# One block with attention and a gated MLP on one Trainium2 core: LayerNorm 1's modulation on transposed x, half of V's lane-matched copies on engines, and a new written order

## The chip, the cores and the metric

The kernel runs on one core of one Trainium2 chip. The metric is device microseconds per execution. Before the change three executions took 297.26, 295.96 and 296.14 us; the median is 296.14 us. A separate, profiled execution took 296.91 us.

## The reference

Everything is bfloat16; x is 2048 tokens by 448 features. A small vector c gives six modulation rows of 448 (shift, scale and gate for each of two halves). The first half is causal attention in a window of 256 tokens with 16 heads of 28 features, the second a gated MLP in which one 2048 by 2048 matrix mixes the tokens.

```python
mod = silu(c) @ w_mod                  # 448 -> 6 rows: sa, ca, ga, sb, cb, gb
h = layernorm(x) * (1 + ca) + sa       # LayerNorm 1 and its modulation
q, k, v = split(h @ wqkv)              # 16 heads of 28
p = softmax(where(0 <= i - j < 256, q @ k.T * 28 ** -0.5, -1e9))
x = x + ga * ((p @ v) @ wo)
h = layernorm(x) * (1 + cb) + sb       # LayerNorm 2 and its modulation
z = gelu_tanh(h @ w_in)                # 1792 columns
z1, z2 = z[:, :896], layernorm(z[:, 896:])
out = x + gb * ((z1 * (w_sp @ z2 + b_sp[:, None])) @ w_out)
```

## The kernel before

The 2048 tokens are 16 tiles of 128 (t for keys and values, j for queries), and four tiles make a block (tb 0 to 3). All matmuls want their contracted dimension on the partitions, so normalised x is transposed into hT (four chunks of features by 2048 tokens).

**The order.** The function first lists every operation with the engines that may do it, its dependencies and a planner's cost. It does not search: a long string, ORDER, names each operation by its number of creation, its engine and its buffer slot, in order. Each engine runs its operations in exactly this order, so an operation that waits holds up all that stand behind it on that engine. SP (SyncE) issues nearly all transfers, in order as well. Planner costs only order the waits; nothing is timed by them on the chip.

**Front (up to about 20 us).** Matmuls with c (L557, L562) give the modulation columns. LayerNorm 1's modulation goes into the weights: `pad` multiplies the q and k weights by 1 + ca while it spreads heads to 32 columns (WQK, L609 and L610), wv is multiplied likewise (L636, L637), and the shift becomes a bias row: `bias` (L619) multiplies sa by the weights, and the result is put into the row of WQK and wv that meets a column of ones in xn. x is normalised to xn (L668, L670, L673) and transposed, for tb 0 and 1 by the TensorE (L718) and a copy to hT (L731, L732), for tb 2 and 3 by transposing transfers from xn to hT (L476). For tb 0 the four q groups are computed chunk by chunk (L746), then the k groups (L758). V comes from L806 into Vaug (copies L810, L811). For tb 3 K comes tile by tile (L793).

**Attention (to about 131 us).** For each query tile j and each half of the heads: scores on the TensorE (L901 for j 0 and 1; from j 2 on L931, L945 and, through QBD, L959), the exponential on ScalarE (L887, 128x2048 and 128x512), a mask product on VectorE (L964), and P times V (L985, called PV below). For j of 2 and more PV reads V from Vaug and also from VX, in which the 64-row halves of V's tiles are put together in four ways (VX index 0 to 3) so that a window's pieces of 64 keys meet. VX of block tb is used first by the PV of j = 4 tb (j = 2 for tb 0). Of its six pieces of 64 partitions, four stay on their partitions (index 0 and 2 on the lower half, 1 and 3 on the upper: lane-matched) and two cross over. All six are written by four transfers for each block (L826 to L829), two of which write two pieces each:

```python
(lambda e, ...: e.dma_start(both(vx(0, 0), 8 * row, n), both(vo(0, a, b), 0, n)), 0),      # L826: index 0 and 2
(lambda e, ...: e.dma_start(vx(0, 64), vo(0, a - 2, b - 2)), 2),                           # L827
(lambda e, ...: e.dma_start(vx(3, 0), vo(64, a, b)), 0),                                   # L828
(lambda e, ...: e.dma_start(both(vx(1, 64), 8 * row, n), both(vo(64, a - 2, b - 2), 0, n)), 2)  # L829: 1 and 3
```

After PV: a transpose (L1000), 1 / sum (L1002), the product (L1003), a transpose into hT (L1006), the output projection (L1010), x1 (L1015), LayerNorm 2, a transposing transfer (L476), modulation (L1035, L1037).

**Rest (131 to 295 us).** z2 (L1100) and z1 (L1146), the token mixing with w_sp, which is transposed by 32 transfers (L476, wspA and wspB; L1169), the bias and the product with z1 (L1173, L1176), the last projection (L1186), the residual (L1196) and one store for each tile (L1201).

Of the kernel before, what the change touches and what calls it, by code (L numbers as in the profile page):

```python
# [5 lines left out]
BF16 = mybir.dt.bfloat16  # L6
# [13 lines left out]
1.a 26.v 35.g 0.s 27.v 28.v 29.v 38.g 39.g 2.a 4.s 36.g 3.a 33.g 30.v 5.s 37.g 57.a 31.v 34.g 32.v 40.g 6.s 7.s 8.s 9.s 10.s 11.s 12.s 152.v 154.v  # L20
41.g 67.p.1 68.p.2 69.p.3 58.p.0 59.a 60.a 53.a 70.p.4 71.p.5 72.p.6 73.p.7 81.p.2 82.p.3 83.p.4 84.p.5 66.p.1 43.g 42.g 163.v 153.v 155.v 156.g 157.g
13.s 161.v 164.v 162.v 165.v 14.s 166.g 158.v 159.v.0 160.a.1 167.v 169.v.2 170.p.2 168.a.3 171.p 172.a 173.a 174.p.3 175.p 122.v 121.v 135.v 142.p.4
134.g 138.a 140.v 137.v 141.v 136.v 143.v 176.a 177.v 139.a 178.p.5.6.7.0 179.p 144.p.1 180.p 182.p 145.a 146.p.1 199.p.2 181.p 186.v 149.a 147.a
200.a 217.v 213.v 215.v 219.v 48.v 216.v 218.v 214.v 220.v 185.a 62.g 61.g 150.g 151.a 148.g 193.p.4 194.a 195.p.3 196.a 183.p 201.p.6 15.s 16.s 187.a
367.p.0 184.p 197.p.1 63.v 221.v 188.v 198.v 55.g 222.g 223.v 51.v 224.g.0 226.g.1 205.p.7 203.p.0 54.g 368.a 371.p.0 206.a 372.a 204.a 123.p.1 65.v
227.v.2 49.v 225.v.3 369.v 125.v 124.v 64.v 389.p.0 228.p.0 128.p.1 229.v 207.p.7 230.p.0 390.a 391.a 394.p.0 202.a 208.a 395.a 396.a 192.s 189.s
190.s 191.s 17.s 18.s 21.s 22.s 209.s 19.s 211.s 210.s 20.s 212.s 129.v 126.p.1 231.v 127.v 373.v 264.v 268.v 46.v 415.p.0 232.p.0 238.p.1 413.p.0
233.a 239.a 234.p.0 236.p.1 414.a.0 237.a 416.a 370.p.0 374.p 419.p.0 265.v 270.v 266.v 45.v 47.v 269.v 271.v 44.v 267.v 235.v 375.v.0 392.v 50.v
254.p.0 246.p.1 421.p.0 393.p.0 272.g 273.g 274.v 276.g.0 420.a.1 397.v 255.v 319.v 439.p.0 398.p 247.a 422.a 440.a.2 244.p.0 441.p.0 248.p.1 445.p.0
245.a 442.a 423.v 417.v 399.v.1 317.v 418.p.0 424.p 250.p.0 447.p.0 318.v 315.v 425.v.2 443.v 320.v 316.v 446.a.3 251.a 448.a 376.v 241.s 242.s 243.s  # L30
240.s 465.p.0 444.p.0 258.p.0 467.p.0 466.a.4 259.a 468.a 278.g.1 277.g.2 132.g 56.g 130.g 275.g.3 249.v 252.p.1 321.v 449.v 322.v 323.v 400.v 253.v
52.v 426.v 280.s 281.s 282.s 279.s 471.p.0 450.p 256.p.0 473.p.0 472.a.0 299.p.1 257.a 474.a 300.a 491.p.0 283.p.0 295.p.1 493.p.0 324.g 401.g.0
451.v.3 325.v 133.g 131.g 377.v.1 402.v 378.v 469.v 284.v 492.a.1 296.a 494.a 403.p.0 404.v 427.v.2 261.s 260.s 24.s 262.s 263.s 497.p.0 285.p.1
499.p.0 379.p.0 498.a.2 286.a 500.a 470.p.0 517.p.0 327.g.0 328.v.1 428.v 329.v.2 380.v 452.v 475.v 289.p.1 287.p.0 519.p.0 476.p 518.a.3 495.v 501.v
405.v 288.v 477.v.1 290.a 520.a 523.p.0 429.p.1 297.p.0 525.p.0 524.a.4 298.a 526.a 406.v 478.v 521.v 527.v 430.v 381.v 496.p.0 543.p.0 502.p 305.p.0
545.p.0 301.p.1 544.a.0 306.a 546.a 549.p.0 479.g.0 453.g.1 326.g.3 454.v 503.v.0 302.v 382.v 307.p.0 303.p.1 551.p.0 550.a.1 431.v 504.v 505.g.2
383.g 407.g 480.v 304.v 432.v 553.v 433.v 506.v 408.g 409.g 410.g.0 434.g 23.s 332.s 292.s 291.s 294.s 25.s 293.s 330.s 331.s 312.s 333.s 522.p.0
308.a 552.a 569.p.0 455.p.1 309.p.0 571.p.0 528.p 570.a.2 310.a 572.a 575.p.0 456.v 481.p.1 577.p.0 507.p.0 576.a.3 578.a 547.v 529.v.2 457.v 530.v
548.p.0 458.v 482.v 508.v 435.v 384.g 531.g.1 459.g 532.v 595.p.0 554.p 338.p.1 597.p.0 533.p.0 460.g 436.g.1 437.g 573.v 411.v 483.v 555.v.1 579.v
484.v 534.v 535.v 536.v 485.v 596.a.4 339.a 598.a 601.p.0 336.p.1 603.p.0 340.p.0 602.a.0 604.a 621.p.0 314.s 313.s 311.s 438.s 337.v 556.v 341.v  # L40
623.p.0 334.p.1 574.p.0 580.p 537.v 599.v 385.g 557.g.0 581.v.3 622.a.1 335.a 624.a 627.p.0 352.p.0 582.v 509.v 605.v 353.v 348.p.1 629.p.0 349.v
386.g.2 486.g 344.s 412.s 345.s 343.s 342.s 461.g 583.g.2 584.v 462.v.1 463.g 510.v 511.g 538.g 600.p.0 628.a.2 630.a 363.s 464.s 647.p.0 346.p.0
585.p.1 649.p.0 558.v 387.v 625.v 388.s 487.v 631.v 648.a.3 347.a 650.a 653.p.0 606.p 655.p.0 559.p.0 654.a.4 656.a 607.v.0 586.v 560.v 539.v 561.v
626.p.0 673.p.0 632.p 633.v.2 562.v 634.v 608.v 350.p.1 675.p.0 351.v 356.p.0 674.a.0 676.a 679.p.0 540.v.0 357.v 635.g.1 563.g 564.g 360.p.1 354.p.0
681.p.0 541.v 488.g.1 609.g.2 680.a.1 636.v 657.v 651.v 361.v 610.v 683.v 355.a 682.a 699.p.0 637.p.0 652.p.0 658.p 701.p.0 700.a.2 702.a 705.p.0
489.g 565.g 784.g 566.g.2 512.g 567.g 365.s 362.s 364.s 542.s 638.v 611.p.1 358.p.0 568.s 587.v 639.v 659.v.1 640.v 641.v 612.v 707.p.0 706.a.3 359.a
708.a 725.p.0 727.p.0 726.a.4 728.a 677.v 642.g 643.v 660.v 588.v 613.v 703.v 678.p.0 684.p 731.p.0 787.g 661.g.0 513.g 614.v 662.v 514.v.0 685.v.3
709.v 686.v 729.v 687.g.1 663.p.1 704.p.0 710.p 733.p.0 732.a.0 734.a 751.p.0 711.v.2 730.p.0 753.p.0 752.a.1 754.a 688.v 712.v 515.v 589.g 735.v
689.p.0 736.p 366.s 490.s 801.s 802.s 516.s 785.g 713.g.2 664.v 615.v 714.v 644.g.2 755.v 757.p.0 759.p.0 715.p.1 758.a.2 790.a 760.a 737.v.0 645.v
756.p.0 786.g 590.g 616.g 690.v 665.v 738.v 739.g.0 761.v 833.p.0 834.p.1 835.p 762.p 791.a 788.a 789.a 666.v 716.v 740.v 717.v 741.p.0 763.v.1 742.v  # L50
764.v 667.g 591.g 592.g.1 593.g 668.g 669.v 617.v 837.a 836.p 691.v 692.v 718.v 618.v.0 646.s 670.v.2 839.v 838.v 619.g 845.a 868.p.2 869.p.3 870.p
871.p 851.p.0 872.a 852.p.1 853.p 854.p 880.a 981.p.2 846.v 671.v 743.v 744.v 745.v 777.g 693.g 694.g 746.g 747.g 594.s 620.s 672.s 719.v 765.v.1
766.v 767.p.0 862.a 840.v 720.g 748.v.1 749.g 863.g 695.v 881.v 750.s 780.g 721.g 696.g.0 792.g 722.g.2 841.v 768.v 874.v 769.v 697.v 770.v 771.g
873.v 793.v 795.v 794.v 882.a.0 855.a 982.p.1 983.p 886.p.3 887.p.0 888.p 889.p 984.p 986.a 985.a 847.a.1 698.s 857.v 883.v 772.g 773.v 723.v 724.s
774.g.1 856.v 775.v 776.s 858.v 799.v 806.s 814.s 813.s 807.s 798.v 875.v 890.a 897.a 987.a 988.a 898.g 842.g 843.g 816.s 804.s 811.s 810.s 805.s
809.s 812.s 815.s 808.s 803.s 899.a.0 779.g 844.g 884.g 783.g 921.p.2 922.p.3 923.p 924.p 864.a.1 797.v 796.v 932.a 903.p.0 904.p.1 865.v 892.v 866.g
# [1212 lines left out]
```

## Time and profile before

| what | value |
|---|---|
| median of three executions | 296.14 us |
| the profiled execution: its time, and the span of its trace | 296.91 us, 295.0 us |
| busy: TensorE, VectorE, ScalarE, GpSimd | 271.4, 158.6, 139.2, 131.1 us |
| mean granted TensorE clock | 0.977 |
| front; attention; z1 and z2; token mixing and output | 0 to 20; 20 to 131.4; 131.4 to 173.5; 173.5 to 295.0 us |

PE is the TensorE, PEld its loading of weights, DVE VectorE, ACT ScalarE, POOL GpSimd, SPq the queue of SyncE. In the chain and in the timeline a line has a start, a duration (both in us), an engine or "issue" (time in which an engine waited for nothing that the profile shows), and the line of the program. An x4 behind it counts instructions. "[3.78 <-DMA VX<-Vaug]" is idle time ahead of an instruction and what ended it.

### The profile page before, as it was taken

How to read it: one execution, taken by the hardware profiler on the slowest of the kernel's cores; microseconds unless marked ns; L12 is line 12 of the kernel's file. 1: busy time of each engine (PE TensorE's matmuls, PEld its weight loads, DVE VectorE, ACT ScalarE, POOL GpSimd, SP SyncE). 2: the span in 40 equal slices, each digit the busy share in tenths (PEclk: the TensorE clock that was granted, in tenths of full speed). 3: DMA queues.
4: the chain of work that ended last, by engine and by line, in shares of the span. 5: the costliest groups of instructions: out<-in, count | busy, mean ns of one | idle time of the engine just before them, and what ended most of it. 6: DMA issues, size and time to landing. Idle time of an engine off the chain costs nothing.

```text
span 295.0 us, 8590 instructions
## 1 busy us (share of the span) xinstructions
PE 271.4 (92%) x3795; PEld 135.4 (46%) x3795; DVE 158.6 (54%) x360; ACT 139.2 (47%) x182; POOL 131.1 (44%) x179
## 2 busy tenths in 40 slices
PE   6999979599999785699999999999999999999995
PEld 2445444245555553344444444444444444444452
DVE  7688996828989697488785600013011024051534
ACT  3688989659999695488999950000000000000000
POOL 6563386006942385376884861006313064252310
PEclk9999999979999998599999999999999999999999
DMA  7927643964774959612399999940000000000123
GB/s 220 297 100 197 140 81 78 213 189 102 152 106 95 108 102 172 94 22 56 66 150 180 168 219 170 195 69 2 0 0 0 2 0 0 0 18 0 62 64 109
DMA packets 58959, 29.50 MB, mean 100 GB/s; under 512 B 48041, under 2 KB 56298, under 8 KB 58922
## 3 DMA queue, kind: packets, MB, share of 16 engines
q1 hardware_dynamic: 58376, 28.26, 48.3%
q10 hardware_dynamic: 546, 0.69, 0.8%
q8 instruction: 30, 0.49, 0.7%
q14 instruction: 7, 0.06, 0.1%
HBM read 9.01 MB, written 1.84 MB: 37 GB/s over the span
## 4 chain that ended last, share of the span: by engine, by line
PE 80%; DMA 6%; DVE 4%; issue 3%; ACT 3%; SPq 1%; POOL 1%; ACTq 0%
PE ps L1169 33%; PE ps L1100 7%; PE ps L1146 7%; PE ps L1186 7%; PE ps L758 5%; PE ps L985 5%; DMA VX<-Vaug 5%; PE ps L1010 4%; PE ps L806 3%; PE ps L931 2%; DMA wmod<-in_w_mod_dram 2%; ACT PW L887 2%; PE ps L959 2%; PE ps L945 1%; PE ps L746 1%
## 5 line engine op out<-in xcount | busy, mean ns | idle before, releaser
L887 ACT ACTIVATE PW<-ps 128x2048 bf16<-128x2048 f32 (+1 forms) x56 | 68.7, 1241 | 21.0 <-PE ps L945 14.1
L1176 POOL TENSOR_TENSOR z1T<-tmpg,z1T 128x512 bf16<-128x512 bf16 x28 | 31.8, 1152 | 77.0 <-DVE tmpg L1173 77.0
L1173 DVE TENSOR_TENSOR tmpg<-ps,bsp_bc 128x512 bf16<-128x512 f32 x28 | 19.0, 689 | 75.5 <-PE ps L1169 65.0
L1169 PE MATMUL ps<-wspB,z 128*128 128x512 bf16 x224 | 50.0, 379 | 0.0
L1169 PE MATMUL ps<-wspA,z 128*128 128x512 bf16 x224 | 49.5, 379 | 0.0
L1169 PEld LDWEIGHTS ps<-wspA,z 128*128 128x128 bf16 x224 | 21.9, 98 | 26.6 <-POOL z L1115 0.4
L1169 PEld LDWEIGHTS ps<-wspB,z 128*128 128x128 bf16 x224 | 21.9, 98 | 26.3
L1003 POOL TENSOR_TENSOR o_sb<-ou,rec_all 128x512 bf16<-128x512 f32 x13 | 15.5, 1198 | 38.3 <-DVE rec_all L1002 33.6
L758 PE MATMUL ps<-hT,WQK 128*128 128x512 bf16 x96 | 25.5, 400 | 0.0
L964 DVE TENSOR_TENSOR PW<-PW,mask 128x1024 bf16<-128x1024 bf16 x28 | 22.3, 808 | 1.2 <-ACT PW L887 1.2
L1100 PE MATMUL ps<-w_in,hT 64*128 64x448 bf16 x224 | 22.0, 349 | 0.4 <-ACT PW L887 0.4
L1146 PE MATMUL ps<-hT,w_in 64*128 64x512 bf16 x196 | 22.0, 376 | 0.0
L1186 PE MATMUL ps<-w_out_g,z1T 128*128 128x448 bf16 x112 | 21.8, 352 | 0.0
L656 POOL TENSOR_TENSOR rs_all<-ve_all,neghalf 128x1 f32<-128x1 f32 (+2 forms) x29 | 18.6, 646 | 3.9 <-DVE ve_all L653 3.2
L1196 DVE TENSOR_TENSOR fin<-ps,x_sb 128x448 bf16<-128x448 f32 x16 | 9.4, 620 | 18.5 <-PE ps L1186 16.8
L648 DVE BATCH_NORM_STATS2 st_all<-x_sb 128x6 f32<-128x448 bf16 x32 | 18.7, 605 | 0.0
L673 POOL TENSOR_SCALAR xn<-x_sb,rs_all,ve_all 128x448 bf16<-128x448 bf16 x18 | 17.3, 961 | 3.0 <-DVE ve_all L660 2.4
L985 PE MATMUL ps<-PW,VX 128*32 128x64 bf16 x896 | 14.3, 199 | 4.6 <-issue 4.5
L985 PE MATMUL ps<-PW,Vaug 128*32 128x128 bf16 x224 | 12.0, 231 | 6.0 <-DMA VX<-Vaug 6.0
L1000 DVE STREAM_TRANSPOSE ou<-ps 128x512 f32<-128x512 f32 x16 | 11.3, 708 | 10.9 <-PE ps L985 10.9
L1154 ACT ACTIVATE z1T<-ps 128x512 bf16<-128x512 f32 x28 | 14.8, 603 | 3.9 <-PE ps L1146 3.7
L1010 PE MATMUL ps<-wo_g,hT 128*128 128x448 bf16 x64 | 16.1, 374 | 0.2 <-issue 0.2
(130 smaller groups left out, 382.0 us busy)
## 6 DMA issues: line engine op xcount, KB each, us to landing
VX<-Vaug SPq DMA_DIRECT2D x6, 512.0 KB, 5.3
VX<-Vaug SPq DMA_DIRECT2D x8, 256.0 KB, 4.1
out_dram<-fin SPq DMA_DIRECT2D x16, 112.0 KB, 1.8
x_sb<-in_A_x_dram SPq DMA_DIRECT2D x3, 448.0 KB, 4.8
wmod<-in_w_mod_dram SPq DMA_DIRECT2D x1, 1344.0 KB, 8.7
w_in<-in_B_w_in_dram SPq DMA_DIRECT2D x1, 1344.0 KB, 10.3
QBD<-qT SPq DMA_DIRECT2D x16, 64.0 KB, 2.5
w_out_g<-in_B_w_out_dram SPq DMA_DIRECT2D x1, 784.0 KB, 5.7
```

The source lines that it names most:

```text
L648: st = [dve(0.62 if True else 0, lambda e, t=t, ci=ci, s=s: e.bn_stats(st_all[:, slot, t, ci, :], s()), deps(t), prio) for ci, s in enumer ...
L758: m = pe(4 * MMS, [lambda e, h=h, g=g, kc=kc, tb=tb: e.matmul(ps[:, h.slot[0], :], lhsT=WQK[:, kc, 4 * g:4 * g + 4, :].rearrange("p a b -> ...
L887: ex = act(xdur, lambda e, out_ap=out_ap, in_ap=in_ap: e.activation(out_ap(), in_ap(), ACT.Exp, scale=SCALE), [s], v - 8.0 + u, takes, tab ...
L964: fk = lambda e, at_w=at_w, cols=cols: e.tensor_tensor(cols(at_w(), [[512, 4], [128, 4], [1, 64]], PW), cols(at_w(), [[512, 4], [128, 4], ...
L985: fns.append(lambda e, hO=hO, hi=hi, qi=qi, V=V, of=of, q0=q0, w=w, first=bi == 0, last=bi == len(pieces) - 1: e.matmul(ps[32 * hi:32 * hi ...
L1010: mo = pe(4 * MMD, [lambda e, h=h, j=j, ch=ch: e.matmul(ps[:, h.slot[0], 0:D], lhsT=hT[:, ch, j * 128:(j + 1) * 128], rhs=wo_g[:, ch, :], ...
L1100: return lambda e, kc, p0, start, stop: e.matmul(ps[:, hs[t % 2].slot[hf], 0:D], lhsT=hT[p0:p0 + 64, kc, t * 128:(t + 1) * 128], rhs=w_in[ ...
L1146: return lambda e, kc, p0, start, stop: e.matmul(ps[:, hs[b // 2].slot[b % 2], :], lhsT=w_in[p0:p0 + 64, kc, ft * 128:(ft + 1) * 128], rhs ...
L1169: m = pe(16 * MMS, [lambda e, h=h, si=si, ft=ft, tb=tb: e.matmul(ps[:, h.slot[0], :], lhsT=z2[:, si, ft * 128:(ft + 1) * 128], rhs=(wspA i ...
L1173: a = dve(0.7, lambda e, h=h, ht=ht, tb=tb: e.tensor_tensor(tmpg[:, ht.slot[0], :], ps[:, h.slot[0], :], bsp_bc[:, tb * 512:(tb + 1) * 512 ...
L1176: u = pool(1.16, lambda e, ht=ht, ft=ft, tb=tb: e.tensor_tensor(z1T[tb][:, ft, :], tmpg[:, ht.slot[0], :], z1T[tb][:, ft, :], ALU.mult), [ ...
L1186: return [lambda e, ft=ft: e.matmul(ps[:, h.slot[0], 0:D], lhsT=z1T[t // 4][:, ft, (t % 4) * 128:(t % 4 + 1) * 128], rhs=w_out_g[:, ft, :] ...
```

## The change

1. LayerNorm 1's modulation leaves the weights. `pad` only copies; `bias`, its twelve matmuls, the copies of its rows, the four products on wv, the cast `sab` and the column of ones go. For tb 0 and 1 each copy of a chunk into hT (ACT or DVE) now multiplies by 1 + ca and adds sa; for tb 1 there are four such copies where there were two wider ones. For tb 2 and 3, where the transfer writes hT directly, four operations on hT in place are added for each block (for tb 2 two on DVE, one each on ACT and POOL; for tb 3 all four on POOL).
2. In tb 0 the groups of the first eight heads, q0, k0, q1, k1, are computed first and chunk by chunk, then q2, k2, q3, k3.
3. VX: for index 0 (lower) and index 3 (upper) an engine copies the lane-matched piece; POOL copies all 128 partitions and the crossing transfer then overwrites half. DVE does one of the two copies in tb 1 and in tb 3, POOL the other six of the eight. Four transfers of one piece each remain for a block. The two that cross wait for the copy of their index.
4. ORDER is new throughout, found with planner costs in which transfers stand in line at 0.2 MB/us. Among its effects: V's last tile stands farther ahead of the first PV that reads VX; the large load of w_in (1344 KB) is issued behind PV of j 1, ahead of the transposes of tb 2, where it was issued at 53.88 us among VX's transfers for tb 1; the two early transposes of wspA move behind the last PV.
5. The last token tile is projected, added and stored in two halves of 224 columns. An unused mask (low3, one small operation) and a path with masks on the TensorE that was switched off go.

```diff
-    t_low = dve(0.15, lambda e: e.tensor_scalar(low3[:], mask3[:], 1.0, 1.0e9, ...), t_mk3, -9.9)
...
-        op = add({eng: (0.6, fn)}, deps, prio, dma=name, lat=mb / 0.26, tail=2.0)
+        op = add({eng: (0.6, fn)}, deps, prio, dma=name, lat=mb / 0.2, tail=2.0)
...
-        return add({"act": (0.52, lambda e: e.activation(to(), of(), ACT.Copy, scale=by)), "dve": (0.45, fn), "pool": (0.8, fn)},
-                   [t_wq[k][kc], t_wqk0, t_p3, t_modA], prio + 0.01 * kc)
+        return add({"act": (0.52, lambda e: e.activation(to(), of(), ACT.Copy)), "dve": (0.24, lambda e: e.tensor_copy(to(), of())),
+                    "pool": (0.6, lambda e: e.tensor_copy(to(), of()))}, [t_wq[k][kc], t_wqk0, t_p3], prio + 0.01 * kc)
...
-    def bias(k, of, to, loads, prio):
-        ...
-        m = pe(4 * MMD, [lambda e, kc=kc: e.matmul(ps[64:65, h.slot[0], 0:D], lhsT=sab[:, kc:kc + 1], rhs=of(kc), ...) for kc in range(DC)], ...)
...
+            for ch in range(DC):          # tb 2 and 3, behind the transposing transfers
+                evs.append(free(
+                    0.82, lambda e, ch=ch, tb=tb: e.activation(hT[:, ch, tb * 512:(tb + 1) * 512], hT[:, ch, tb * 512:(tb + 1) * 512], ACT.Identity,
+                                                              bias=modT[:, ch:ch + 1], scale=modT[:, 4 + ch:5 + ch]),
+                    0.45, 0.95, lambda e, ch=ch, tb=tb: e.tensor_scalar(hT[...], hT[...], modT[:, 4 + ch:5 + ch], modT[:, ch:ch + 1], ALU.mult, ALU.add),
+                    [ts, t_modA], v + ch * 0.1))
...
+            for k in range(2):            # tb 0 and 1, out of PSUM
+                ch = 2 * cp + k
+                ev = either(0.77, lambda e, ...: e.activation(hT[...], pst(h, k * 512, (k + 1) * 512), ACT.Identity, bias=..., scale=...),
+                            0.55, lambda e, ...: e.tensor_scalar(hT[...], pst(h, k * 512, (k + 1) * 512), ..., ALU.mult, ALU.add),
+                            m + [t_modA] + evs[2 * cp:], v + cp * 0.1)
...
+            first = (0, 4, 1, 5)
+            hq = {g: Hold(bA) for g in first}
...
+        for k, p0, q0, back in ((0, 0, 64, 0), (3, 64, 0, 2)):
+            need = [t_va, [V_ready[t] for t in range(a - back, b - back)]]
+            same = add({"dve": (0.1 + 0.16 * (b - a), lambda e, ...: e.tensor_copy(vx(k, p0, p0 + 64), vo(p0, p0 + 64, a, b))),
+                        "pool": (0.1 + 0.57 * (b - a), lambda e, ...: e.tensor_copy(vx(k, 0, 128), vo(0, 128, a, b)))}, need, v)
+            for n, (k2, to, of, first) in enumerate(((k, q0, p0, other), (2 - k // 3, p0, p0, a - back))):
+                V_half[tb].append(add({"sp": (0.6, lambda e, ...: e.dma_start(vx(k2, to, to + 64), vo(of, of + 64, first, first + n)))},
+                    [t_va, [V_ready[t] for t in range(first, first + b - a)], t_vz[tb % 2] if n else same], v, dma=name, lat=0.34 * (b - a), tail=2.1))
...
     for tb in range(2, NB4):
+        for d in V_half[tb]:
+            d.deps.update(all_PV[8 * tb - 16:8 * tb - 8])
...
+            for c0, c1 in ((0, D // 2), (D // 2, D)) if t == NT - 1 else ((0, D),):
```

More of the change, by code (lines that the diff above doesn't have):

```diff
@@ L613, in bass_adaLN_cond__sliding_block__mixer_gmlp__prompt_kernel @@
     t_wqk = [[pad(kc, k, -49.5 + 0.2 * k) for kc in range(DC)] for k in range(2)]
-    def bias(k, of, to, loads, prio):
-        h = Hold(bA if k == 0 else bM)
-        m = pe(4 * MMD, [lambda e, kc=kc: e.matmul(ps[64:65, h.slot[0], 0:D], lhsT=sab[:, kc:kc + 1], rhs=of(kc), start=(kc == 0), stop=(kc == DC - 1),
-                                                   tile_position=(0, 64)) for kc in range(DC)], [t_sab, loads], prio, [h])
-        row = lambda: ps[64:65, h.slot[0], 0:D]
-        return h, m, row
@@ L624, in bass_adaLN_cond__sliding_block__mixer_gmlp__prompt_kernel @@
-    t_bias = []
-    for k in range(2):
-        h, m, row = bias(k, lambda kc, k=k: wq_st[:, kc, D * k:D * k + D], None, [t_wq[k], t_p3], -49.0 + 0.2 * k)
-        to = lambda k=k: WQK[64:65, 3, H * k:H * k + H, 0:DH]
-        cp = add({"act": (0.55, lambda e, to=to, row=row: e.activation(to(), row().rearrange("p (h d) -> p h d", d=DH), ACT.Copy)),
-                  "dve": (0.63, lambda e, to=to, row=row: e.tensor_copy(to(), row().rearrange("p (h d) -> p h d", d=DH)))}, [m, t_wqk[k][3]], -48.9 + 0.2 * k)
-        h.until.append(cp)
-        t_bias.append(m)
-        t_wqk[k].append(cp)
@@ L641, in bass_adaLN_cond__sliding_block__mixer_gmlp__prompt_kernel @@
-    h.until.append(cp)
-    t_wvs.append(cp)
     def stats(slot, tiles, srcs, deps, prio, shift=True):
```

255 lines of the change are left out of this document (111 added, 144 removed).

## The prediction

> **What bounds the kernel now.** I read the busy shares first, then the stretches of the kernel one by one, then the chain of waits, then the TensorE's timeline around each gap. By the page's first part the TensorE is busy 92% of the span; the busy time of each stretch tells where the other 8% lies.
>
> ```profile
> PE 271.4 (92%) x3795; PEld 135.4 (46%) x3795; DVE 158.6 (54%) x360; ACT 139.2 (47%) x182; POOL 131.1 (44%) x179
> ```
> ```profile
> 60.00:64.30 4.30, 4.30 (x79) 1.70 (x61) 0.06 (x1) 2.42 (x2) 0.00 (x0) 0.60 0.94 254
> 64.30:92.00 27.70, 27.28 (x894) 16.09 (x893) 24.54 (x52) 25.75 (x26) 16.22 (x22) 1.00 0.56 108
> ...
> 121.00:125.70 4.70, 4.45 (x128) 2.26 (x117) 3.73 (x9) 3.07 (x3) 2.54 (x3) 0.53 0.32 68
> ...
> 131.40:173.50 42.10, 42.10 (x407) 19.76 (x406) 27.92 (x84) 36.12 (x66) 31.87 (x58) 1.00 0.76 131
> ```
>
> Columns: stretch, length, busy us of PE, PEld, DVE, ACT, POOL, granted clock, DMA share, GB/s. From 131.4 us on the TensorE has no gap until its last matmul ends at 291.6: there only less TensorE work would help, and the change takes none away. All that can be won lies before. An undisturbed stretch of attention (64.3 to 92) has PE at 98%, ACT at 93% and DVE at 89%, so nothing can run much faster than that pace. The rest is gaps, and the chain names them:
>
> ```profile
> 12.80 0.85 PE ps L619 x4
> 13.64 1.19 PE ps L746 x5
> 14.83 0.86 PE ps L619 x4
> ...
> 53.22 6.45 DMA VX<-Vaug
> ...
> 60.76 3.44 PE ps L758 x8
> ...
> 106.48 6.85 DMA VX<-Vaug
> ...
> 117.14 3.54 issue
> ```
> ```profile
> 29.16 1.89 PE L758 MATMUL ps<-hT,WQK 128*128 128x512 bf16 x8
> ...
> 59.71 0.24 PE L985 MATMUL ps<-PW,Vaug 128*32 128x128 bf16 x4 [3.78 <-DMA VX<-Vaug]
> ...
> 113.42 0.24 PE L985 MATMUL ps<-PW,Vaug 128*32 128x128 bf16 x4 [2.17 <-DMA VX<-Vaug]
> ```
>
> Two bias products stand in the front's chain. PV of j 4 waits 3.78 us and PV of j 12 waits 2.17 us for VX. Behind the first wait eight L758 matmuls take 3.44 us on the chain where eight take 1.73 us at 29.32: the granted clock is 0.60 there, and 1.71 us are lost besides the wait.
>
> **Part 1, modulation.** Removed from the TensorE: three groups of four bias matmuls, 0.86 us each on the chain. The first group (9.81 to 10.7) fills time in which the TensorE would wait for hT and WQK anyway (L746 starts at 10.91 after a wait for WQK), so two groups count: 2 x 0.86 = 1.7 us less. The wv products (L636, 2.78 us on POOL) go too, off the path. Bounds: 0, if the k weights, whose transfers are issued last and which the first eight heads now need at once, keep the TensorE waiting; 3.2 us, if the scores of j 0 (19.77 now) start as early as q0, k0, q1 and k1 let them, about 16.6. I take 1.7, since the TensorE is 10.64 of 11 us busy between 9 and 20, so only removed work shortens it. The copies of hT with modulation are priced as the nearest rows, 0.59 us (L731) to 0.80 us (L1035), against 0.42 to 0.59 for plain ones; other chunks' matmuls cover them.
>
> Added for tb 2 and 3: eight in-place operations. DVE 0.39 to 1.20 (L1037), ACT 0.80 (L1035), POOL 0.77 to 1.28. For tb 2 they run on three engines between the transposes' landing and k1 of tb 2: about 1 us, up to 5 if the transposes land late; I take +1. On ACT the operation stands ahead of the large exponential of j 5, so that this one and all scores behind it would wait. For tb 3 the first user stands many matmuls later, cost nothing, at most the 4 x 1.28 = 5.1 us of POOL if that cover were gone.
>
> **Part 2, VX.** Transfers fall from six pieces to four, from 1.5 to 1 MB a block. Each hand-over now is: V's last copy, an engine copy, the issue, the landing. No row shows POOL copying 2048 columns. By L1037 it is 4 x 0.77 = 3.1 us to 4 x 1.28 = 5.1 us, by L1115 (896 columns in 1.33 us) 3.0; I take 3.0, the nearest row in length. The new order gives cover; I add the TensorE's steps in it from rows (L758 group 0.86, L806 0.76, L931 with L945 0.49, L959 0.22, L985 0.46, L1010 0.86, L793 0.90):
> - tb 1, V of tile 6 to PV of j 4: 11.4 us (before 6.9, with the wait behind it). Chain: copy 0.62 + POOL 3.0 + issue 0.6 + landing 4.1 (the 256 KB row) = 8.3. No wait.
> - tb 2, tile 9 to PV of j 8: 14.1 us. ACT has an exponential ahead (1.88), copy 0.54, two POOL copies 6.0, 0.6, 4.1 = 13.1. No wait, by 1 us.
> - tb 3, tile 12 to PV of j 12: 10.0 us. 1.88 + 0.54 + 3.0 + 0.6 + 4.1 = 10.1. A wait of 0.1; with copies or landings at their upper rows up to 6.9 (5.1 and 8.8, the longest landing of a VX transfer, instead of 3.0 and 4.1), I take +1.5.
>
> So of the waits now 3.78 and 1.71 (clock) and 2.17 go: 7.7 us less. The copies on DVE (two, by the mask's row L964 0.63 to 1.53) and on POOL lie beside TensorE work; POOL is busy 16.2 of 27.7 us in the good stretch. SP issues 16 transfers as before, but each crossing one stands in SP's queue and holds up the transposes of LayerNorm 2 behind it, which nobody needs for some tens of us.
>
> **Part 3, order.** The gap of 3.54 us at 117.14 lies inside a block of PV matmuls, so no semaphore ended it; it starts while the two early wspA transposes are issued:
>
> ```profile
> 115.20 4.86 SPq L476 DMA_TRANSPOSE wspA<-in_B_w_sp_dram x2
> ```
>
> All longer "issue" gaps (1.57 at 42.28, 2.05 at 96.75) lie within 5 us of transposes too. In the new order these two stand behind the last PV, where the TensorE has no gap even at a DMA share over 1 (150 to 173 us). With them would go 3.5 us and the slow clock behind (PE steps from 115.0 to 125.8 take 6.4 us where the same steps cost 3.8 elsewhere): 6.1. As other transposes remain in attention, I take half, 3.0. The other "issue" gaps, 5.6 us in all, I leave. Closer packing bares ACT, at 93% in the best stretch, and any link that I can't see: +2 (0 to 4).
>
> **The last tile.** The second half's add is about half of 0.62 us, seven more weight loads cost 7 x 0.1 at most. I put this at 0, bounds -0.3 to +0.7. [...]
>
> **Sum.** -1.7 - 7.7 - 3.0 + 1 + 1.5 + 2 = -7.9 us. The profiled execution, 296.91 us (span 295.0 and 1.91 around it), would take 289.0; it stands 0.77 above the median, so the median goes from 296.14 to 288.2 us. I say 288.
>
> **Rivals.** Full gain: the half I withheld comes and the three added terms are nothing: 296.14 - 1.7 - 7.7 - 6.1 = 280.6. For it: every added term has cover by rows. Against: new orders have gaps of their own. 0.10.
>
> w_in ahead of the transposes: its 1344 KB took 10.3 us to land, and it is now issued some 16 us of TensorE steps ahead of k1 of tb 2, with four transposes (7.07 us to issue before) behind it. 10.3 + 7.07 = 17.4, and 1 for the modulation: 2.4 late, 4 if the landing of the last (3.0) isn't hidden, with 1.7 for the slow clock: 288.2 + 5.7 = 293.9. For it: ACT is held up as well. Against: x was normalised only at 43.3 us before, so that the 7.07 us hold waiting. 0.18.
>
> Slower, POOL's hand-over: it decides once POOL's copies come at 1.28 us per 512 columns and stand behind about two other POOL operations (2.5 us). Then the chains are 12.9, 19.8 and 14.7 us against covers of 11.4, 14.1 and 10.0: waits of 1.5, 5.7 and 4.7, with 1.7 of slow clock behind the two long ones 15.3 in all. Instead of the 1.5 I took, 288.2 + 13.8 = 302.0. It turns the change slower from about 9.5 us of waits on. For it: POOL is in order, and its copies stand among products (L1003, 1.20 us) and roots. Against: POOL was idle 41% of the good stretch. The mask rows show DVE and POOL slowing each other:
>
> ```profile
> L964 DVE TENSOR_TENSOR PW<-PW,mask x28: 627/680/1529, 37.4 to 128.7; 128x1024 bf16<-128x1024 bf16 x28
> ```
>
> Such a product takes 627 ns at least and 1529 at most. [...] 0.30 for this case. That the change doesn't do what it says I put at nothing: names and order show the copies and the removed matmuls.
>
> **Numbers.** The forecast has 0.42. A measurement of this kernel can tell about 0.5% (1.5 us). Faster by more: forecast, full gain and two thirds of the w_in case: 0.42 + 0.10 + 0.12 = 0.64; within: 0.06; slower: 0.30. The likeliest case alone spans 282 to 293. The range goes from 280, under the full gain, to 301, which leaves out half of the slower case (0.15) and some 0.03 below.
>
> **What would show it.** Right: no L619; the first L931 before 30.98; no wait for VX over 1 us at PV of j 4; granted clock 1.00 from 60 to 64; no gap over 3 us in attention; L1169 starting near 165.5 where it starts at 173.53. Wrong: PV (L985) waiting for VX over 2 us at j 8 or j 12 with a POOL copy ending late; L1035 or k1 of tb 2 waiting for hT<-xn; the gaps of "issue" as long as now in spite of the moved wspA; L1169 waiting for wspA.

## The result and the profile after

The kernel after took 288.43 us (median of four executions, 286.50 to 290.03), the kernel before 296.05 in the same comparison (295.85 to 297.26): a ratio of 0.9731, 95% interval 0.9666 to 0.9797. The forecast was 288.0. Ratios, here and below, are of fast executions alone (within 1.5% of the kernel's fastest), while the times beside them are medians of all. The profiled execution took 288.54 us, span 286.8, where before had 296.91 and 295.0. A right total can stand on wrong terms, so I took the span apart by the starts of score blocks (the first matmuls of L931 before, L897 after; j and half as in the order), the first mixing product (L1169, now L1124) and the end:

| stretch | before, us | after, us | change |
| --- | --- | --- | --- |
| start to scores j 5, half 1 | 53.43 | 55.17 | +1.74 |
| to j 7, half 1 (PV of j 4 lies here) | 17.20 | 13.23 | -3.97 |
| to j 12, half 0 | 25.57 | 27.02 | +1.45 |
| to j 15, half 1 | 29.95 | 20.12 | -9.83 |
| to the first mixing product | 47.38 | 50.85 | +3.47 |
| to the end | 121.51 | 120.43 | -1.08 |
| sum | 295.04 | 286.82 | -8.22 |

More than the whole net gain falls between j 12 and j 15, where the prediction had placed about 5 us of it. The stretches do not hold the same work in both kernels: between j 12 and j 15 the TensorE has 723 matmuls before and 672 after, between j 7 and j 12 806 and 906. Of the 9.83 us, 5.63 are idle time of the TensorE that is gone (9.13 to 3.50), the other 4.20 are busy time: work that stands elsewhere now, and a clock that went from 0.83 to 1.00. Over the whole span the idle time fell from 23.65 to 19.35 us and the busy time from 271.39 to 267.47. The waits of the TensorE after (waiting line, releaser, us in total, times, longest):

```profile
PE ps L938 <- issue: 3.6, 6, 1.3
...
PE ps L731 <- DVE hT L681: 1.6, 1, 1.6
PE ps L938 <- DVE ve_all L615: 1.3, 1, 1.3
PE ps L897 <- ACT PW L855: 1.1, 2, 0.9
```

No wait for a VX transfer is left (L938 is PV, L985 before), and no gap over 1.3 us is put down to issue, where 3.54 was the longest. New is the first line of DVE: k1 of tb 2 (L731) waits 1.64 us for the in-place modulation (L681). The stretches, with the columns of the prediction:

```profile
60.00:64.30 4.30, 4.09 (x133) 2.49 (x134) 4.23 (x8) 3.78 (x5) 1.34 (x2) 1.00 0.49 69
64.30:92.00 27.70, 26.42 (x851) 15.68 (x853) 25.54 (x52) 24.98 (x26) 19.66 (x25) 1.00 0.36 83
106.00:114.00 8.00, 6.22 (x221) 3.44 (x218) 8.00 (x19) 7.58 (x7) 6.91 (x10) 1.00 0.25 31
```

The clock is 1.00 from 60 to 64.3, as forecast, and the DMA share 0.49 where it was 0.94. But in the undisturbed stretch DVE is busy 25.54 of 27.7 us where it was 24.54, POOL 19.66 where it was 16.22, and from 106 to 114 DVE has no idle time at all. The chain of waits names what that does (start, us, what):

```profile
29.16 1.68 PE ps L588 x4
...
116.58 1.38 DVE PW L917
118.03 0.81 PE ps L938 x38
118.85 3.43 PE ps L1055 x22
```

The mask products (L917) stand on the chain, and the z2 products (L1055) start at a lowered clock, 0.64 from 118.85 to 122.28 us: 22 take 3.43 us.

### The profile page after: what moved, and what is told of

It is laid out like the page before. It is cut to its first block, busy times and chain, and to the rows that moved or that the text cites. A ratio compares the mean times of both kernels' runs of the same rounds, so it can differ in the third digit from the quotient of the medians.

```text
span 286.8 us, 8569 instructions
## 1 busy us (share of the span) xinstructions
PE 267.5 (93%) x3770; PEld 135.5 (47%) x3795; DVE 168.1 (59%) x372; ACT 133.0 (46%) x170; POOL 140.5 (49%) x189
## 4 chain that ended last, share of the span: by engine, by line
PE 74%; DVE 14%; ACT 5%; issue 3%; POOL 2%; DMA 1%; ACTq 0%
PE ps L1124 33%; PE ps L1143 7%; PE ps L1055 6%; PE ps L731 6%; PE ps L938 4%; PE ps L779 3%; PE ps L963 3%; PE ps L897 2%; PE ps L1101 2%; DVE st_all L610 2%; PE ps L912 2%; DVE PW L917 2%; ACT fin L1087 1%; PE ps L903 1%; PE ps L766 1%
## 5 line engine op out<-in xcount | busy, mean ns | idle before, releaser
L1124 PE MATMUL ps<-wspB,z 128*128 128x512 bf16 x218 | 49.2, 379 | 0.3
L1124 PE MATMUL ps<-wspA,z 128*128 128x512 bf16 x219 | 48.4, 379 | 0.8 <-DVE z L1073 0.6
L1124 PEld LDWEIGHTS ps<-wspA,z 128*128 128x128 bf16 x224 | 21.8, 98 | 27.0 <-DVE z L1073 0.9
L1124 PEld LDWEIGHTS ps<-wspB,z 128*128 128x128 bf16 x224 | 21.9, 98 | 26.1
L731 PE MATMUL ps<-hT,WQK 128*128 128x512 bf16 x83 | 21.9, 387 | 3.3 <-DVE hT L681 1.6
L1055 PE MATMUL ps<-w_in,hT 64*128 64x448 bf16 x224 | 23.5, 363 | 0.0
L917 DVE TENSOR_TENSOR PW<-PW,mask 128x1024 bf16<-128x1024 bf16 x28 | 23.4, 842 | 0.0
L1153 DVE TENSOR_TENSOR fin<-ps,x_sb 128x448 bf16<-128x448 f32 (+1 forms) x17 | 9.7, 593 | 22.5 <-PE ps L1143 21.8
L1143 PE MATMUL ps<-w_out_g,z1T 128*128 128x448 bf16 (+1 forms) x119 | 22.3, 341 | 0.1
L938 PE MATMUL ps<-PW,VX 128*32 128x64 bf16 x896 | 13.9, 195 | 3.6 <-issue 3.6
L1143 PEld LDWEIGHTS ps<-w_out_g,z1T 128*128 128x128 bf16 x119 | 11.6, 98 | 10.2
L1055 PEld LDWEIGHTS ps<-w_in,hT 64*128 64x128 bf16 x224 | 10.9, 97 | 11.4 <-issue 2.3
L1101 PEld LDWEIGHTS ps<-hT,w_in 64*128 64x128 bf16 x196 | 9.5, 94 | 11.5 <-ACT z1T L1109 0.3
L635 POOL TENSOR_SCALAR xn<-x_sb,rs_all,ve_all 128x448 bf16<-128x448 bf16 x17 | 14.1, 831 | 1.3 <-DVE ve_all L622 1.0
```

The lines of the kernel that those rows point to most:

```text
L731: m = pe(4 * MMS, [lambda e, h=h, g=g, kc=kc, tb=tb: e.matmul(ps[:, h.slot[0], :], lhsT=WQK[:, kc, 4 * g:4 * g + 4, :].rearrange("p a b -> ...
L917: fk = lambda e, at_w=at_w, cols=cols: e.tensor_tensor(cols(at_w(), [[512, 4], [128, 4], [1, 64]], PW), cols(at_w(), [[512, 4], [128, 4], ...
L938: fns.append(lambda e, hO=hO, hi=hi, qi=qi, V=V, of=of, q0=q0, w=w, first=bi == 0, last=bi == len(pieces) - 1: e.matmul(ps[32 * hi:32 * hi ...
L1055: return lambda e, kc, p0, start, stop: e.matmul(ps[:, hs[t % 2].slot[hf], 0:D], lhsT=hT[p0:p0 + 64, kc, t * 128:(t + 1) * 128], rhs=w_in[ ...
L1101: return lambda e, kc, p0, start, stop: e.matmul(ps[:, hs[b // 2].slot[b % 2], :], lhsT=w_in[p0:p0 + 64, kc, ft * 128:(ft + 1) * 128], rhs ...
L1124: m = pe(16 * MMS, [lambda e, h=h, si=si, ft=ft, tb=tb: e.matmul(ps[:, h.slot[0], :], lhsT=z2[:, si, ft * 128:(ft + 1) * 128], rhs=(wspA i ...
```

## The experiments

All ratios are to the kernel before, run on the same chip as the kernel beside it. Three chips were used, on which the kernel before had medians of 298.4 to 298.8 us, so ratios are compared, not times. Each kernel left one trace, of one execution; what two traces show apart can differ by the execution too. My theory at the start was that of the prediction: shorter waits for VX and no early wspA transposes. The rivals were the writing of VX by itself, the cover in the order by itself, and something that neither names. Edits of the order are written with the operations' names: S a block of scores, Smid its middle part, DMAT a transposing transfer, ld a load, ev a copy out of PSUM.

### Where the two wspA transposes stand

```diff
 order on SP, kernel before
-DMAT h2 j4, DMAT wspA 0, DMAT wspA 1, DMAT h2 j5, DMAT h2 j10, DMAT h2 j8, ..., DMAT h2 j14
+DMAT h2 j4, DMAT h2 j5, DMAT h2 j10, DMAT wspA 0, DMAT h2 j8, ..., DMAT wspA 1, DMAT h2 j14
```

> The kernel before, with one edit of its order: the two early transposes of wspA move on SP's queue behind the last PV (ahead of the LayerNorm 2 transposes of tiles 8 and 14), as the change has them. If these two starve the TensorE of its instructions (the prediction's part 3), the 3.54 us gap and the slow clock behind it go: 290, between 287 and 293. If that gap has to do with something else (the other transposes, the number of small PV matmuls) it stays or moves: 295 to 297.

Measured: 298.11 us, ratio 0.9963 (0.9906 to 1.0019). The gaps stay: issue adds up to 9.8 us where it was 9.1. The longest shrinks to 1.87 us, at 121.02, and one of 2.49 appears at 80.91. The reverse edit on the kernel after puts both transposes early again:

```diff
 order on SP, kernel after
+DMAT h2 j4, DMAT wspA 0, DMAT wspA 1
-DMAT h2 j4
```

> The changed kernel, with the two wspA transposes early again: right behind the LayerNorm 2 transpose of tile 4 on SP's queue. By the first theory a gap of 3 us or more with a slow clock comes back ahead of the end of attention: 291 to 295. By the other 288.4, within 1.5.

Measured: 289.62 us, ratio 0.9711 (0.9624 to 0.9799), no loss against 0.9731, though its trace has a gap of 1.77 us at 115.65 that the kernel after lacks. Part 3 of my prediction falls: the long gap did not hang on these two transposes alone.

### How VX is written

```diff
 kernel before, its order kept
-4 transfers a block: two of 512 KB (two pieces each), two of 256 KB
+2 engine copies (POOL or DVE as after) and 4 single transfers
```

> The kernel before in its own order, with VX as the change makes it (two engine copies and four single transfers for each block, the copies on the change's engines and ahead of the place of the old transfers). If the smaller transfers are what takes the waits for VX away: the waits of 3.78 and 2.17 us shrink by half or more, 291 to 294. If it is the new order's longer cover (V's last tile 6.9 us ahead in this order, 11.4 in the new one), the chain of copy and transfer, 8.3 us by the prediction, still ends later than its cover: the waits stay, or grow by the POOL copies, 295 to 299.

Measured: 300.57 us, ratio 1.0181 (1.0135 to 1.0227), slower. The TensorE now waits for VX three times:

```profile
PE ps L981 <- DMA VX<-Vaug: 9.3, 3, 5.4
```

In the old order the copies only add a link to the hand-over: 9.3 us of waits where there were 6.0. The counterpart takes the copies out of the kernel after:

```diff
 kernel after, its order kept
-2 engine copies and 4 single transfers a block
+4 transfers a block as before, no copies
```

> The changed kernel in its own order, with VX by the four transfers of before (two of them write two pieces) and without the engine copies. If the cover is what counts: no wait for VX over 1 us, 288.4 within 1.5, or up to 1 us less since DVE and POOL lose 2 and 6 copies. If the smaller transfers count: a wait of 2 us or more at PV of j 4 or j 12, 291 to 296.

Measured: 290.73 us, ratio 0.9736 (0.9634 to 0.9839); its trace has no wait for VX either. So the engine copies, the change's headline, bring nothing that these runs can tell (about one per cent either way). The new order brings the gain with either way of writing VX. Something does change without the copies: the wait of 1.64 us for the modulation is gone (its cause follows in the part on the prediction), while gaps of issue come to 8.1 us where the kernel after has 4.5. The version with wspA early has 7.8 us of them, and its time can't be told from these two either: the sum of such gaps by itself is no measure of time.

### More TensorE work ahead of PV

If the order helps by the work that it lays ahead of PV, then that should work in the kernel before too:

```diff
 TensorE order, kernel before
-PV j4.0, S j6.0, q3 tb2, q2 tb2, Smid j6.0, PV j4.1, S j6.1, wo j2, k1 tb2
+S j6.0, q3 tb2, q2 tb2, Smid j6.0, k1 tb2, wo j2, PV j4.0, PV j4.1, S j6.1
-PV j12.0, PV j12.1, S j14.1, wo j11
+S j14.1, wo j11, PV j12.0, PV j12.1
```

> The kernel before with six words of its order moved and nothing else: the products k1 of tb 2 and wo of j 2 ahead of both halves of PV of j 4, both halves of PV of j 4 behind the scores and Q/K products around j 6, and PV of j 12 behind the second scores of j 14 and wo of j 11. TensorE work laid ahead of PV of j 4: 0.49 + 0.86 + 0.86 + 0.22 + 0.86 + 0.86 = 4.15 us against a wait of 3.78; ahead of PV of j 12: 0.49 + 0.86 = 1.35 against 2.17. Theory (what removed the waits for VX is the TensorE work that the order puts ahead of them; how VX is written matters little): the wait at j 4 under 0.5 us, that at j 12 near 0.8, the clock at 1.00 behind j 4, and 3.78 + 1.71 + 1.35 = 6.8 us less at most, a ratio of 0.977 to 0.985. Rival (the transfers themselves are late, by the queue or by their size, and shift with the rest): waits of 2 us or more stay and the ratio is 0.995 to 1.00.

Measured: 298.77 us, ratio 0.9990 (0.9940 to 1.0040). The waits for VX are gone, as the theory said, and nothing is won. The TensorE's timeline behind j 6 shows who took their place (idle time before the row, and its releaser, in brackets):

```profile
59.37 1.04 PE L757 MATMUL ps<-hT,WQK 128*128 128x512 bf16 x4 [1.10 <-DVE qT L768]
...
64.56 0.38 PE L930 MATMUL ps<-qT,KT 32*64 32x128 bf16 x32 [1.11 <-ACT PW L886]
...
66.39 0.31 PE L944 MATMUL ps<-qT,KT 32*64 32x128 bf16 x2 [1.29 <-issue]
67.40 1.67 PE L805 MATMUL ps<-wv,hT 128*128 128x448 bf16 x4
```

A copy out of PSUM, an exponential and a gap of issue come to 3.5 us, and four V products behind them take 1.67 us, at a clock of 0.66 from 65 to 70 us; in the kernel after, at 1.00, four take 0.93. The scores of j 7, half 1 start at 70.45 us; in the kernel before they start at 70.63. The opposite edit on the kernel after:

```diff
 orders of TensorE and VectorE, kernel after
-V t6, wo j1, PV j3.0, PV j3.1, S j5.0, k1 tb2, Smid j4.0, q3 tb2, S j5.1, Smid j4.1
+wo j1, PV j3.0, PV j3.1, S j5.0, k1 tb2, Smid j4.0, q3 tb2, S j5.1, Smid j4.1, V t6
+ev V t6 and the VX copy of tb 1 on VectorE behind it
```

> The kernel after with the V product of tile 6, its copy to SBUF and VectorE's copy of VX of tb 1 moved behind wo of j 1, PV of j 3, k1 and q3 of tb 2 and the scores between: 0.86 + 0.90 + 0.49 + 0.86 + 0.22 + 0.86 + 0.49 + 0.22 = 4.9 us of the cover ahead of PV of j 4 are gone. In the kernel after the last transfer of VX of tb 1 is issued at 54.6 us, lands by some 59.6 at the latest, and PV of j 4 starts at 62.6: about 3 us to spare. Theory (cover decides): a wait for VX of about 2 us at PV of j 4, 0 to 1.7 us of slow clock behind it, ratio to the kernel before 0.98 to 0.987 where the kernel after has 0.973. Rival (the engine copies and the single transfers decide): no wait for VX over 0.5 us, ratio 0.97 to 0.977.

Measured: 289.72 us, ratio 0.9630 (0.9526 to 0.9734), no wait for VX. The expected 2 us did not come; the TensorE waited 0.72 and 1.54 us for copies of V out of PSUM instead. PV of j 4 starts at 62.17 us, about when it does in the kernel after (62.66), but 10.85 us behind the scores of j 5, half 1, where it is 7.49 there: the cover was partly made good by these waits. The ratio rests on two executions, and the trace is of another. The run doesn't support cover as the deciding term, and it can't exclude it.

### The modulation alone

```diff
 kernel before
-bias products, products on wv, modA folded into WQK
+hT multiplied and shifted: tb 0, 1 in the copies from PSUM, tb 2, 3 in place (tb 2: ACT, POOL, DVE, DVE)
```

> The kernel before with the modulation of LayerNorm 1 alone as it is after: on the transposed x, with no bias products, and no other part of the change; four in-place modulations for tb 2 ahead of its k2 product, four for tb 3 on POOL. Theory of the prediction: two groups of bias products of 0.86 us off the front's path, 1 us of waits for the modulation at tb 2, so -0.7 us, ratio 0.99 to 1.00, the first scores near 18.0 us where they start at 19.77. What the kernel after showed (the 1.75 us won at j 0 are lost by j 2 to a slower clock): the scores of j 2 start no earlier than in the kernel before, ratio 1.00 to 1.01. Rival (the modulations load VectorE and POOL where they are scarce, and the gain of the change is made in spite of them): ratio over 1.01.

Measured: 302.01 us, ratio 1.0108 (1.0009 to 1.0208). The front gains what was forecast: scores of j 0 start at 18.15 us (19.77 before) and of j 2 at 29.67 (30.98). Then it is lost, more than once:

```profile
PE ps L937 <- issue: 6.7, 5, 3.6
PE ps L896 <- issue: 4.2, 2, 3.1
PE ps L726 <- POOL hT L679: 3.2, 1, 3.2
```

The added modulation on POOL is waited for 3.2 us in this order, and gaps of issue come to 10.9 us. The ratio lies at the edge between what the kernel after had led me to expect (1.00 to 1.01) and the rival (over 1.01), and the interval covers both. The waits for VX are down to 0.5 us in this trace, from 6.0, and again nothing is won.

### The last tile

```diff
 kernel after
-last tile added and stored in two halves of 224 columns
+last tile whole
```

> The kernel after with its last tile whole: one add and one store of 112 KB for tile 15 in place of two halves, and the halves' separate products put back together. By the prediction 0 (bounds: the halves win 0.3 or lose 0.7), ratio to the kernel before 0.97 to 0.976 as the kernel after. Rival, from the two traces: the halves win about 1 us, since the time from the first mixing product to the end fell from 121.5 to 120.4 us; then this kernel is 0.6 to 1.1 us slower than the kernel after, ratio 0.975 to 0.98, and the last store starts later behind the last matmul.

Measured: 289.87 us, ratio 0.9704 (0.9616 to 0.9793), not to be told from the kernel after. In the traces, the first mixing product to the end takes 120.89 us with the whole tile and 120.43 with halves: the halves win about 0.5 us. Five traces with halves and this tail lie between 120.43 and 120.66, so 0.2 to 0.5 us are theirs, and the rest of the 1.08 I put down to the order of the tail.

### What the gaps of issue are

So far two things stood out: every trace has gaps that no semaphore ended, and they move when anything else is moved. The profile of before has a small queue that I had passed over (its page's queue rows; then the same rows for 113.0 to 118.2 us, where the gap begins, and for 118.2 to 120.7, where it ends; packets, MB, share of 16 engines):

```profile
q8 instruction: 30, 0.49, 0.7%
```
```profile
q1 hardware_dynamic: 1987, 1.06, 100.7%
q14 instruction: 1, 0.01, 1.1%
```
```profile
q1 hardware_dynamic: 1089, 0.27, 110.5%
q8 instruction: 1, 0.02, 2.8%
```

Thirty packets of 16 KB make 0.49 MB, 65 bytes for each of the 7590 matmuls and weight loads. I read q8 as the TensorE's own instructions, fetched by the DMA engines while the kernel runs. In the gap of 3.54 us (117.15 to 120.69) the packet starts at 118.33 and ends at 119.47. Over the fourteen traces of this study, all 76 TensorE gaps of 0.4 us or more put down to issue lie between 20 and 135 us, and all end 1.19 to 1.67 us after the end of such a packet; packets come some 5 us apart there, so chance would give about one in ten.

A count says more. Number the TensorE's instructions in order: each weight load together with its matmul (eight of the traces lack 25 or 26 records of matmuls), and the three or four dozen semaphore and drain instructions. If n packets have landed by then, the matmul that ends the gap is number 256n + 194 or 256n + 195, in all 76 gaps. The orders of these kernels differ, and of the 79 gaps of that length that are put down to another engine, 5 lie at these two of the 256 places. So in each of the 76 the TensorE stands at the end of one packet's instructions until the next packet has landed.

The pace is seen where nothing disturbs it (two windows from one packet's start to the next's; the third and fifth numbers count matmuls and weight loads):

```profile
111.48:118.33 6.85, 3.67 (x159) 2.25 (x160) 4.40 (x8) 3.57 (x3) 3.52 (x5) 0.77 1.09 163
...
233.08:260.24 27.16, 27.16 (x130) 12.58 (x129) 6.41 (x10) 0.00 (x0) 10.13 (x9) 1.00 0.00 1
```

In the quiet end a packet comes every 130 + 129 = 259 instructions; ahead of the gap 319 pass between two, and the former was late already. Counted from the start, with semaphore and drain instructions, packet n begins at instruction 256n - 99 in the quiet end (packet 29 at 7325) and at 256n + 193 ahead of this gap (packet 19 at 5057), some 290 late. By the count above no packet of the fourteen traces begins later than 256n + 194, and seven begin at 193 or 194: by then the TensorE has stopped at the place found above. The 290 are one packet's 256 instructions and some three dozen more, the most that a packet comes late in these traces. What sets that limit, no run shows.

A small matmul is the hungry one: between 111 and 126 us the kernel before issues a packet's worth in 3.5 to 4 us where it can, at the end in 26 to 28. Late packets stop the TensorE in attention alone, and ahead of this gap the data queue (q1) takes all 16 engines' time. The load of w_out was issued at 112.87 us, ahead of the longest gap. That gives an experiment:

```diff
 order on SP, kernel before
-DMAT h2 j7, ld wout, DMAT h2 j4, ..., DMAT h2 j15
+DMAT h2 j7, DMAT h2 j4, ..., DMAT h2 j15, ld wout
 order on POOL: four of w_out's seven products with the gate behind a later one
```

> The kernel before with the load of w_out (784 KB, issued at 112.87 us) moved behind the last transpose of LayerNorm 2, and four of its seven products with the gate moved behind a later one on POOL; nothing else. All profiles so far show a 16 KB packet of the TensorE's instruction queue landing up to 2.3 us ahead of the end of each TensorE gap put down to issue; ahead of the gap of 3.54 us at 117.14 that packet starts only at 118.33, 449 instructions after the place where such packets start in the quiet end of the kernel is overrun by some 290. Theory (the packet stands behind data on the DMA engines, here behind the 784 KB): the gap at 117 falls under 1.5 us and the slow clock behind it goes in part, 3 to 5 us less, ratio 0.983 to 0.99. Rival (the transposes alone hold the packet up, or the gap has another cause): a gap of 2 us or more stays between 110 and 125, ratio 0.995 to 1.00.

(The 449 of that text is a slip of counting; the row above has 159 + 160 = 319.) Measured: 294.57 us, ratio 0.9872 (0.9823 to 0.9921), as the theory said. The gap shrinks to 0.45 us and another of 1.29 follows at 120.46:

```profile
118.02 0.22 PE L984 MATMUL ps<-PW,VX 128*32 128x64 bf16 x5 [0.45 <-issue]
```

One load, whose first matmul starts 140 us later (252.8 in the kernel before), brings nearly half of the change's gain. With the later PV of the earlier run:

```diff
 kernel before
+both edits: PV j 4 and j 12 later, ld wout later
```

> The kernel before with the six moved words of the run with more cover (PV of j 4 and of j 12 later) and the late load of w_out together. Theory (waits for VX and late instruction packets each take the other's place, so that both have to go): more than the sum of the two alone, 5 to 7 us less, ratio 0.976 to 0.985, near the whole of the change. Rival (something else, such as the pace of VectorE and ScalarE, sets the time between): ratio over 0.99.

Measured: 297.15 us, ratio 0.9878 (0.9807 to 0.9949): the late load alone. The theory that both have to go together is not borne out. A gap of 1.77 us at 96.8 stands in this trace as one of 1.93 does in that with the late load alone:

```profile
99.07 0.24 PE L944 MATMUL ps<-qT,KT 32*64 32x128 bf16 x2 [1.93 <-issue]
```

It lies behind VX's transfers of tb 3 and two transposes of LayerNorm 2. To tell them apart, the last run takes away bytes and keeps all else:

```diff
 kernel before with ld wout late
-row, n = H * 32, (b - a) * H * 32
+row, n = H * 32, 32 if tb == 3 else (b - a) * H * 32
 and the other two transfers cut to [:, :n]
```

> The kernel before with the late load of w_out, and the four VX transfers of tb 3 cut to one head's 32 columns each (4 KB a transfer in place of 256 and 512 KB; the rest of that VX buffer keeps the values of tb 1, so this part of V is left out for j 12 to 15). Orders, waits and the number of transfers are as in the run with the late load alone, which has a gap of 1.93 us at 97.1 put down to issue, 0.75 at 107.2, a wait of 1.98 at PV of j 12, and a ratio of 0.987. Theory (the bytes of VX of tb 3 hold up both PV of j 12 and the instruction packets): the gap at 97 falls under 1 us, the wait at PV of j 12 under 0.5, 3 to 4 us less, ratio 0.973 to 0.98. Rival (the transposes of LayerNorm 2 that stand beside these transfers hold the packet up, and VectorE's chain holds PV of j 12): gap and wait stay, ratio 0.985 to 0.99.

Measured: 289.66 us, ratio 0.9771 (0.9668 to 0.9874). The gap at 97 shrinks to 0.84 us, the wait at PV of j 12 is gone:

```profile
97.17 0.24 PE L944 MATMUL ps<-qT,KT 32*64 32x128 bf16 x2 [0.84 <-issue]
```

Side by side, the window from 96.2 to 126.2 us in the kernels before, with the late load, with the late load and small VX, and after (PE busy is the first number behind the length; clock, DMA share and GB/s are the last three):

```profile
96.20:126.20 30.00, 20.87 (x731) 13.19 (x732) 21.21 (x46) 18.45 (x17) 16.20 (x21) 0.83 0.78 115
```
```profile
96.20:126.20 30.00, 22.55 (x854) 14.46 (x850) 24.44 (x53) 21.43 (x21) 18.68 (x24) 0.94 0.63 96
```
```profile
96.20:126.20 30.00, 25.77 (x862) 15.85 (x858) 27.89 (x65) 25.68 (x26) 21.13 (x30) 1.00 0.34 53
```
```profile
96.20:126.20 30.00, 24.97 (x798) 14.68 (x795) 28.26 (x63) 23.35 (x21) 22.39 (x32) 0.94 0.43 79
```

As the DMA share falls from 0.78 to 0.34, TensorE, VectorE and ScalarE all get more done and the clock returns (0.83, 0.94, 1.00). Scores of j 12 to j 15, half 1 take 29.95, 26.27, 22.00 and 20.12 us. Without two groups of transfers the old order gains 7.95 us in this stretch, where the kernel after gains 9.83; that it gains them in the same way is not shown, since its stretch holds other work. The intervals of the two runs overlap (0.9823 to 0.9921, 0.9668 to 0.9874), so what the small VX adds rests on the traces, the gap and the wait above. The kernel after reaches its time with all its bytes: VX of tb 3 is issued from 92.5 to 96.5 us in one go, and w_out at 113.73, shortly before the last scores (115.54); 80 small PV matmuls still follow, the last at 122.54, among larger ones. The kernel after with w_out or the transfers of VX back at their old places was not run, so which part of the new order wins stays open.

### A version with the late load on top

```diff
 order on SP, kernel after
-DMAT h2 j6, ld wout, DMAT h2 j7, ..., DMAT h2 j15
+DMAT h2 j6, DMAT h2 j7, ..., DMAT h2 j15, ld wout
 order on POOL: three of w_out's products with the gate behind a later one
```

> The kernel after with the load of w_out (784 KB, issued at 113.73 us) behind the last transpose of LayerNorm 2 and three of its products with the gate behind a later one. The kernel after has a clock of 0.79 between 115 and 120 us and DMA engines 95% busy there. Theory (late instruction packets): PE busier between 115 and 121, 0.5 to 2 us less than the kernel after, ratio to the kernel before 0.966 to 0.972. Rival: the products z2 wait for the transposes anyway, ratio as the kernel after, 0.972 to 0.976.

Measured: 287.60 us (286.32 to 290.10), ratio 0.9663 (0.9598 to 0.9728); its profile has a span of 284.6 us and a clock of 1.000. The interval overlaps that of the kernel after (0.9666 to 0.9797), and the version with less cover has 0.9630 on two executions: it is among the best here, not shown to be better than the kernel after.

## Why the prediction was right, and where it was not

**Modulation, -1.7.** Right at j 0, which starts 1.75 us earlier (18.02), and in the run with the modulation alone down to j 2. In the kernel after it is gone by j 2, 1.79 us later than before (32.77, 30.98), and the sign that I had named, the first L931 before 30.98, failed. Four L588 products there take 1.68 us, at a granted clock of 0.50. In five other traces with this front the same four take 0.93 (three of them), 1.42 and 1.48, and j 2 starts between 30.63 and 32.83. So the clock belongs to the execution or the chip, and even where it is full (0.93, j 2 at 31.42 in the version with the late load) the 1.75 us are gone by j 2.

The +1 for tb 2 measured 1.64, and in the old order 3.2. The size was near by luck, for in the kernel after its cause is not the one that I gave:

```profile
49.49 0.41 DVE L681 TENSOR_SCALAR hT<-hT,modT 128x512 bf16<-128x512 bf16 x1
...
50.31 2.05 DVE L681 TENSOR_SCALAR hT<-hT,modT 128x512 bf16<-128x512 bf16 x1
50.33 1.89 POOL L797 COPY VX<-Vaug 128x2048 bf16<-128x2048 bf16 x1
...
52.72 0.81 PE L731 MATMUL ps<-hT,WQK 128*128 128x512 bf16 x3 [1.64 <-DVE hT L681]
```

VectorE's first in-place product takes 0.41 us; the second, of the same shape, takes 2.05 and ends with the copy of VX that runs beside it on POOL. In the version without the copies, its order kept, it takes 0.40, the wait is gone, and the scores of j 5, half 1 start at 51.27 us where they start at 55.17. In the versions with wspA early and with the last tile whole it takes 2.05 again.

**VX, -7.7, and the hand-over, +1.5.** The waits went as forecast and the clock behind them returned (0.60 to 1.00 from 60 to 64.3 us), but the step "so many us of waits gone, so many us won" failed. The 5.49 us (3.78 and 1.71) at j 4 are gone from the kernel after, but its stretch is 3.97 shorter; in the run with more cover the wait is gone too, and the same stretch takes 17.33 us where it took 17.20. The tb 3 hand-over cost no wait. POOL's copy, priced at 3.0 us, takes 1.89:

```profile
L797 POOL COPY VX<-Vaug x6: 1036/1888/1892, 27.4 to 94.1; 128x2048 bf16<-128x2048 bf16 x4, 128x1024 bf16<-128x1024 bf16 x2
...
L796 DVE COPY VX<-Vaug x2: 749/924/1100, 52.4 to 93.0; 64x2048 bf16<-64x2048 bf16 x2
```

The rows I took had two operands or a scale; this plain copy is faster, 0.92 ns a column where L1115 took 1.48 (1.33 us for 896). With it the waits for VX in the rival where POOL's hand-over makes the kernel slower had no ground. In the mean POOL's copies hardly slow VectorE: 28 mask products take 842 ns where they took 808. But the product above was held by one, and the TensorE waited 1.64 us for it: the rival's reason, that POOL and VectorE slow each other, did cost time, at a place that I had not looked at. Of the 28 mask products in the trace of before, the eight over 0.8 us (0.81 to 1.53) all run beside work on POOL, and the eight with none beside them take 0.63 to 0.68; the other twelve have POOL beside them and take 0.63 to 0.69.

**wspA, -3.0.** The place was right, the cause wrong. I blamed the transfer that was being issued when the gap began; the packet that ended it was in another queue, behind data issued 4 us earlier. The order did win in that stretch: 9.83 us, where my terms for it (2.17 for the VX wait and 3.0) make 5.2; a part of the difference is work that moved out of the stretch. One figure in the working is off: the steps from 115.0 to 125.8 add up to 7.0 us, not 6.4, which would have made the term 3.3.

**Other links, +2.** Too small: 1.45 us are lost between j 7 and j 12, where VectorE and POOL carry more, and 3.47 between the last scores and the first mixing product. Of the latter some 1.3 us are the clock (22 L1055 products take 3.43 us at 0.64, the next 28 in the same chain 2.75 at 1.00); the rest I have not traced, and moved work is a part of these figures as well.

So the sum of -7.9 met -8.22 by terms that cancel; that the total came so close is luck in good part. Measured less forecast: the front to j 5 +2.4 (+1.74 against -1.7 and +1), the stretch of PV j 4 +1.5, the other links +2.9, j 12 to 15 -4.7, the hand-over of tb 3 -1.5, the tail -1.1.

**The tail, 0.** The halves are worth 0.2 to 0.5 us in the traces, at most 0.2 beyond my bound, and no timing can tell. The smaller stores land no sooner, 2.1 us for 56 KB against 1.7 for 112:

```profile
out_dram<-fin SPq DMA_DIRECT2D x15, 112.0 KB, 1.7
...
out_dram<-fin SPq DMA_DIRECT2D x2, 56.0 KB, 2.1
```

**w_in ahead of the transposes.** It landed in 7.1 us where it took 10.3, and no link waited for it. Whether its old place, issued at 53.88 us among the VX transfers of tb 1, explains the stretch of j 5 to j 7 as w_out does the end of attention, was not tried.

## What to carry to other kernels

Where many small matmuls run, look at the instruction queues in the profile's queue part, and at where their packets lie against gaps that no semaphore ends. Then move large transfers with late users out of that stretch before touching the work itself: w_out's late load alone gave a ratio of 0.9872. And a wait on the critical path need not bring its length when it goes: in the run with more cover 6.0 us of waits for VX went and nothing was won. Take it away alone before it is put into a sum.

## What the runs showed of the hardware that I had not expected

The TensorE's instructions share the DMA engines with data: a 16 KB packet takes 0.9 to 1.4 us in the kernel before. In all 76 gaps the TensorE stops at the end of one packet's instructions, for up to 3.6 us, and resumes 1.2 to 1.7 us after the next packet ends. A plain bf16 copy of 128x2048 on POOL takes 1.89 us, 0.92 ns a column, and such a copy held a bf16 product of VectorE for its length: 2.05 us where the product takes 0.40 without the copy. The lowered clock at the front (0.50, four products in 1.68 us; 0.93 to 1.48 in five other traces with the same front) follows idle times of 0.25 and 0.42 us; its cause stays open.
